# Eight kinds of matrix product written as four side-by-side strips of 32 output rows, in a two-part attention kernel whose order a planner sets

## The chip, the core and the metric

The kernel runs on one core of one Trainium2 chip. The metric is the device time of one execution in microseconds (us); the time before is the median of three runs. A profile records one further execution, instruction by instruction, on the core's engines: TensorE (PE, with the weight loads apart as PEld), VectorE (DVE), ScalarE (ACT), GpSimd (POOL), and SyncE (SP), whose queue issues most of the transfers.

## The reference

Two independent halves read their own `x` of 2048 rows by 512 columns, and their outputs are placed side by side. Half A is softmax attention with 32 query heads of width 16 that share one key and one value head. Half B is linear attention with a softmax feature map.

```
A:  q = x @ wq  (32 heads x 16),  k = x @ wk,  v = x @ wv  (16 columns each)
    p = softmax(q k^T / 4) over 2048 keys;   out_A = (p @ v) @ wo
B:  q, k, v = x @ wqkv  (32 heads x 16 each)
    phi(t) = [softmax(t w_phi), softmax(-t w_phi)]         (32 features per head)
    kv = phi(k)^T v,  z = sum of phi(k) over the rows
    out_B = (phi(q) kv / (phi(q) z + 1e-6)) @ wo
out = [out_A, out_B]
```

Half A holds nearly all of the work: 32 heads x 2048 x 2048 exponentials.

## The kernel before

**Half A, scores.** A unit is 128 keys against 512 queries of one head. Its score product has a contraction over 32 rows (16 of them hold zeros for the other head of a pair), so four units stand in the four row strips of the array side by side (`score`, line 1694, called "row" form below). Four units with the same keys block make a quad; there are 512 quads. A quad takes one of two ways:

- The ACT way (371 quads). Units are gathered into score groups of three and of two in turn (`next_qk`, `qk`); three PSUM banks hold a group of three and two others a group of two. One ACT instruction does the exponentials of a whole group, 128x1536 or 128x1024 (`expo`, line 1758), and frees its banks for the group after next. Then `pv` (line 1803) multiplies a quad by the values: four products with 32 output rows each, side by side in the column strips ("col" form).
- The DVE way (141 quads). DVE turns the scores into half-precision bit patterns (`bits`, line 1867, one 128x512 piece for each unit), derives three shifted copies of a quad (line 1886 on DVE, line 1883 on POOL, where POOL's copy waits for DVE's copies of the same quad), and `d_sums` (line 1924) sums them with the values in 16 col-form products. The program of a DVE quad is `next_dq` and `d_pv`.

**Half B and the projections.** These are products with all 128 rows and 128 columns of the array ("full" form), four accumulating steps of 512 columns each, or two for `b_q4`: `proj_q` (line 1684, 15 times), `outproj` (line 1992, 12), `b_pk` (line 2158, 16), `b_projv` (line 2187, 16), `b_pq` (line 2255, 16), `b_q4` (line 2325, 16), `b_s8` (line 2342, 16). Each writes one of two or three spare PSUM banks; DVE copies the result away, or ACT applies an exponential (line 2166 for keys, line 2262 for queries, twice for each bank).

**What sets the order.** A planner in the kernel (`run`, `ready`, `issue`) keeps a clock for each engine, gives every job a duration, a form, a due time and a priority, and writes the instructions of all engines in the order of its plan. The chip gets each engine's list in that order, and semaphores between them. The planner charges 0.105 us where a TensorE job's form differs from the one before (`SWITCH`). It also follows how busy TensorE was lately (`active`, `weight`) and puts in products of zeros (`fill`, line 1450, and `company`, line 1433), which accumulate nothing, where it holds TensorE for too idle. `SEEDS` has a number for each 14 us of the plan: it jitters the priorities there (`rank`) and chooses some of the planner's thresholds.

**The end.** The last query block's result is finished in `finish_last`: after the last `pv` a chain of two shuffles on DVE, logarithm and exponential on ACT, a product on DVE, the last products with `wo` (lines 2012 and 2049), copies, and three transfers. DVE and SP branch there on a flag that says whether the inputs were in range.

Of the kernel before, what the change touches and what calls it, by code (L numbers as in the profile page):

```python
# [1174 lines left out]
class _Fast:  # L1175
# [180 lines left out]
    def issue(self, j, start):  # L1356
# [79 lines left out]
    def fill(self, cols=(512,), start=False, mode="full", bank=None):  # L1436


        ps, zero = self.ps, self.zero
        if bank is None:  # L1440
            bank = self.ACC
        r, m = (32 if mode == "row" else 128), (32 if mode == "col" else 128)

        def fn(pe):
            mm = None
            for n in cols:
                rhs = self.ones[0:r].unsqueeze(1).to_broadcast([r, n // 128, 128])
                for x in range(0, 128 if mode == "col" else 32, 32):
                    kw = {} if mode == "full" else dict(tile_position=(0, x))
                    mm = pe.matmul(ps[x:x + m, bank, 0:n].rearrange("p (a n) -> p a n", n=128), lhsT=zero[0:r, 0:m], rhs=rhs, start=start, stop=start, **kw)  # L1450
# [105 lines left out]
    def jobs_a(self):  # L1556
# [28 lines left out]
        for qt in range(12):  # L1585
            job(("op", qt), "pe", 0.87, (lambda qt: (lambda: self.outproj(qt)))(qt), mode="full", nb=1, prio=3.5, after=[("on", qt // 4 * 8 + a) for a in range(1, 8, 2)])
            job(("oa", qt), "dve", 0.60, (lambda qt: (lambda: self.outproj2(qt)))(qt), after=[("op", qt)], frees=[("op", qt)], prio=1)
# [87 lines left out]
    def proj_q(self, ch):  # L1675
# [306 lines left out]
    def outproj(self, qt):  # L1982

        ps, On = self.ps, self.On
        P = qt // 4 * 4
# [3 lines left out]
        def fn(pe):  # L1989
            mm = None  # L1990
            for A in range(4):
                mm = pe.matmul(ps[:, bank, :], lhsT=On[:, (P + A) % 6, q0:q0 + 128], rhs=self.wo2[:, A, :], start=(A == 0), stop=(A == 3))  # L1992
            return mm
# [95 lines left out]
    def jobs_b(self, t0, t1):  # L2089
# [12 lines left out]
        for st in range(16):  # L2102
            job(("bk", st), "pe", 0.87, self.b_pk, after=[("wfc", 1, dc) for dc in range(4)] + ([("kv", st - 2)] if st > 1 else []), mode="full", nb=1, prio=3, rel=at(st))
# [4 lines left out]
            job(("bv", st), "pe", 0.87, self.b_projv, after=[(self.BVA, st)], mode="full", nb=1, prio=3)  # L2108
            job(("vs", st), "dve", 1.13, self.b_vs, after=[("bv", st), ("rs", st)], frees=[("bv", st)], prio=1)
# [3 lines left out]
        for m in range(4):  # L2113
            for G in range(4):
                w = [("s8", 4 * (m - 2) + i) for i in range(4)] if m > 1 else [("wf", k, dc) for k in range(2) for dc in range(4)] if m == 0 else []
                job(("bq", m, G), "pe", 0.87, self.b_pq, after=[("wfc", 0, dc) for dc in range(4)] + w, mode="full", nb=1, prio=3,
                    rel=at(15 + 4.5 * m + G))
# [10 lines left out]
            for C in range(4):  # L2128
                job(("q4", m, C), "pe", 0.44, self.b_q4, after=[("ew", m, s) for s in range(2)], mode="full", nb=1, prio=3, rel=at(19 + 4.5 * m + 0.5 * C))
                job(("q4d", m, C), "dve", 0.60, self.b_q4d, after=[("q4", m, C)], frees=[("q4", m, C)], prio=1)  # L2130
        for st in range(16):
            m = st // 4
            job(("s8", st), "pe", 0.87, self.b_s8, after=[("q4d", m, C) for C in range(4)], mode="full", nb=1, prio=3, rel=at(20 + 4.5 * m + 0.9 * (st % 4)))
            job(("s8c", st), "dve", 0.60, self.b_s8c, after=[("s8", st)], frees=[("s8", st)], prio=1)
# [16 lines left out]
    def b_pk(self, st):  # L2151
# [3 lines left out]
        def fn(pe):  # L2155
            mm = None
            for dc in range(4):
                mm = pe.matmul(ps[:, bank, :], lhsT=xT[:, dc, st * 128:(st + 1) * 128], rhs=w[:, dc, :], start=(dc == 0), stop=(dc == 3))
            return mm
# [20 lines left out]
    def b_projv(self, st):  # L2180
# [3 lines left out]
        def fn(pe):  # L2184
            mm = None
            for dc in range(4):
                mm = pe.matmul(ps[:, bank, :], lhsT=xT[:, dc, st * 128:(st + 1) * 128], rhs=w[:, dc, :], start=(dc == 0), stop=(dc == 3))  # L2187
            return mm
# [59 lines left out]
    def b_pq(self, m, G):  # L2248
# [3 lines left out]
        def fn(pe):  # L2252
            mm = None
            for dc in range(4):
                mm = pe.matmul(ps[:, bank, :], lhsT=w[:, dc, G * 128:G * 128 + 128],  # L2255
                               rhs=xT[:, dc, m * 512:(m + 1) * 512], start=(dc == 0), stop=(dc == 3))
            return mm
# [59 lines left out]
    def b_q4(self, m, C):  # L2317
# [3 lines left out]
        def fn(pe):  # L2321
            mm = None
            for sg in range(2):
                G = 4 * sg + C
                mm = pe.matmul(ps[:, bank, :], lhsT=KVn[:, G, :], rhs=ET[:, (8 * m + G) % 16, :], start=sg == 0, stop=sg == 1)  # L2325
            return mm
# [7 lines left out]
    def b_s8(self, st):  # L2334
# [4 lines left out]
        def op(pe):  # L2339
            mm = None  # L2340
            for C in range(4):
                mm = pe.matmul(ps[:, bank, :], lhsT=ET[:, (8 * m + C) % 16, i * 128:i * 128 + 128], rhs=self.Bwo[:, C, :], start=(C == 0), stop=(C == 3))
# [21 lines left out]
    SEG = 14.0  # L2364
    SEEDS = (984051, 95131, 273450, 658257, 663488, 424264, 0, 164647, 270549, 733254, 842970, 0, 1027032, 574002, 1003492, 900138, 838487,
# [3 lines left out]
    PVN = 2  # L2369
# [227 lines left out]
```

## Time and profile before

| | |
|---|---|
| median of three runs | 722.78 us (722.75 to 723.17) |
| time of the profiled execution | 722.69 us |
| its span, first to last instruction | 720.9 us |
| mean granted TensorE clock | 0.999 |
| ACT busy | 707.5 us, 98% of the span |
| PE busy | 679.1 us, 94% |
| DVE busy | 667.0 us, 93% |
| POOL busy | 397.2 us, 55% |

Busy time alone does not say which engine sets the end: three engines are above 90%. ACT's instructions overlap at their ends, and PE's busy time holds the products of zeros. A row `L1758 ACT ACTIVATE f_PT<-f_ps` is the exponential of line 1758, which reads the PSUM tile `f_ps` and writes `f_PT`. A shape such as `128*32 128x512` stands for a product with 128 contraction rows and 32 columns of the array, over 512 columns of the moving operand. In the chain of waits a piece gives its start, its length, and what stood there; in a timeline, the bracket at a row's end is the idle time of that engine ahead of it, with what ended it.

### The profile page before, as it was taken

What the parts mean: (1) busy time and instruction counts of PE and PEld (TensorE: products, weight loads), DVE (VectorE), ACT (ScalarE), POOL (GpSimd) and SP (SyncE); (2) the same over time, 40 slices, a digit from 0 to 9 for tenths busy, and PEclk for the clock granted to TensorE, in tenths of its full rate; (3) what the DMA queues carried; (4) which work ended last, traced back from release to release, by engine and by line L of the source; (5) the groups of instructions that cost most, each with busy time, mean ns of one, the idle gap of its engine ahead of it and who ended that gap; (6) DMA issues with size and microseconds to landing.
All of it is one profiled execution on the core that took longest, in us unless ns stands there. A gap on an engine that the chain in (4) does not pass through costs nothing.

```text
span 720.9 us, 17413 instructions
## 1 busy us (share of the span) xinstructions
PE 679.1 (94%) x7415; PEld 214.6 (30%) x7415; DVE 667.0 (93%) x1101; ACT 707.5 (98%) x666; POOL 397.2 (55%) x291
## 2 busy tenths in 40 slices
PE   9989999999999999999999999999999999999997
PEld 3223323333332232222233222323232232232322
DVE  4999999999999999998999999999999999899995
ACT  6999999999999999999999999999999999999996
POOL 6455646646454564666546456566464466444551
PEclk9999999999999999999999999999999999999999
DMA  9920000000000100000012310100003010040101
GB/s 184 152 79 25 3 9 17 1 25 2 10 17 27 29 2 10 16 3 24 3 42 49 83 38 2 40 9 16 17 2 100 21 43 13 4 118 2 25 30 35
DMA packets 45539, 23.91 MB, mean 33 GB/s; under 512 B 35405, under 2 KB 41549, under 8 KB 45453
## 3 DMA queue, kind: packets, MB, share of 16 engines
q1 hardware_dynamic: 43724, 22.43, 13.5%
q8 instruction: 59, 0.97, 0.6%
q10 hardware_dynamic: 1728, 0.30, 0.2%
q14 instruction: 28, 0.22, 0.1%
HBM read 10.27 MB, written 4.96 MB: 21 GB/s over the span
## 4 chain that ended last, share of the span: by engine, by line
ACT 96%; PE 3%; DMA 1%; DVE 0%; issue 0%
ACT f_PT L1758 91%; ACT f_ET L2262 2%; ACT f_Ek L2166 2%; DMA f_AxT<-in_A_x_dram 1%; PE f_ps L1694 1%; PE f_ps L1924 1%; PE f_ps L2012 1%; PE f_ps L1803 0%; PE f_ps L1992 0%; PE f_ps L1621 0%; DVE f_outA L1456 0%; PE f_ps L1607 0%; PE f_ps L2325 0%; PE f_ps L2049 0%; PE f_ps L1450 0%
## 5 line engine op out<-in xcount | busy, mean ns | idle before, releaser
L1758 ACT ACTIVATE f_PT<-f_ps 128x1536 bf16<-128x1536 f32 x594 | 682.1, 1391 | 0.8 <-PE f_ps L1694 0.7
L1883 POOL TENSOR_TENSOR f_Zt<-f_Z,f_step 128x1024 int32<-128x1024 int32 x187 | 353.7, 1892 | 285.4 <-DVE f_Zt L1886 262.9
L1867 DVE TENSOR_SCALAR f_Z<-f_ps 128x512 int16<-128x512 f32 x564 | 366.4, 681 | 22.2 <-PE f_ps L1694 18.6
L1694 PE MATMUL f_ps<-f_QA,f_KR 32*128 32x512 bf16 x2048 | 300.0, 384 | 32.8 <-ACT f_PT L1758 23.1
L1886 DVE TENSOR_SCALAR f_Zt<-f_Z 128x2048 int16<-128x2048 int16 x236 | 164.0, 717 | 0.2
L1694 PEld LDWEIGHTS f_ps<-f_QA,f_KR 32*128 32x128 bf16 x2048 | 78.1, 91 | 273.7 <-ACT f_PT L1758 187.0
L1803 PE MATMUL f_ps<-f_PT,f_VA 128*32 128x512 bf16 x1484 | 122.2, 386 | 0.4 <-DVE f_accS L1456 0.3
L1924 PE MATMUL f_ps<-f_Zt,f_VK 128*32 128x512 f16 x1692 | 115.7, 379 | 0.0
L1450 PE MATMUL f_ps<-f_ones,f_zero 128*128 128x512 bf16 (+10 forms) x248 | 59.7, 350 | 1.3 <-POOL f_zero L1476 1.3
L1924 PE MATMUL f_ps<-f_Z,f_VK 128*32 128x512 f16 x564 | 56.3, 389 | 0.1
L1924 PEld LDWEIGHTS f_ps<-f_Zt,f_VK 128*32 128x32 bf16 x1692 | 45.1, 97 | 31.5
L1803 PEld LDWEIGHTS f_ps<-f_PT,f_VA 128*32 128x32 bf16 x1484 | 26.7, 94 | 58.5 <-issue 55.0
L1433 PE MATMUL f_ps<-f_ones,f_zero 32*128 32x512 bf16 x75 | 26.9, 380 | 0.0
L1450 PEld LDWEIGHTS f_ps<-f_ones,f_zero 128*128 128x128 bf16 (+2 forms) x248 | 17.0, 97 | 26.6 <-issue 22.2
L1924 PEld LDWEIGHTS f_ps<-f_Z,f_VK 128*32 128x32 bf16 x564 | 14.5, 93 | 33.5 <-issue 29.5
L1456 DVE COPY f_accS<-f_ps 128x512 f32<-128x512 f32 x31 | 21.3, 686 | 3.4 <-PE f_ps L1924 2.2
L1980 POOL TENSOR_TENSOR f_On<-f_accS,f_denS 128x512 bf16<-128x512 f32 x14 | 17.8, 1272 | 6.4 <-DVE f_Zt L1886 4.5
L2262 ACT ACTIVATE f_ET<-f_ps 128x512 bf16<-128x512 f32 x32 | 20.8, 816 | 0.0
L2166 ACT ACTIVATE f_Ek<-f_ps 128x512 bf16<-128x512 f32 x32 | 20.3, 787 | 0.0
L2172 DVE TENSOR_REDUCE f_ssum<-f_Ek 128x64 f32<-128x1024 bf16 x16 | 19.4, 1210 | 1.0 <-ACT f_Ek L2166 0.9
L2197 DVE TENSOR_TENSOR f_vS<-f_ps,f_rs 128x1024 bf16<-128x1024 f32 x16 | 19.5, 1219 | 0.6 <-PE f_ps L2187 0.6
L2255 PE MATMUL f_ps<-f_BxT,f_Wq 128*128 128x512 bf16 x64 | 16.6, 382 | 0.4 <-DVE f_Z L1867 0.2
(108 smaller groups left out, 324.8 us busy)
## 6 DMA issues: line engine op xcount, KB each, us to landing
f_denS<-f_dd SPq DMA_DIRECT2D x15, 256.0 KB
out_dram<-f_outB SPq DMA_DIRECT2D x17, 128.0 KB, 2.3
f_Wk<-f_wd SPq DMA_DIRECT2D x4, 512.0 KB
f_Ek<-f_wd SPq DMA_DIRECT2D x4, 512.0 KB
f_accS<-f_accS SPq DMA_DIRECT2D x60, 32.0 KB
out_dram<-f_outA SPq DMA_DIRECT2D x14, 128.0 KB, 1.8
f_Bwv<-in_B_wqkv_dram SPq DMA_DIRECT2D x1, 512.0 KB
f_Bwo<-in_B_wo_dram SPq DMA_DIRECT2D x1, 512.0 KB
```

The lines of the kernel that those rows point to most:

```text
L1433: self.add("pe", lambda pe: pe.matmul(out, lhsT=zero[0:32, :], rhs=rhs, start=False, stop=False, tile_position=(0, 0)), reads=["ones", "ze ...
L1450: mm = pe.matmul(ps[x:x + m, bank, 0:n].rearrange("p (a n) -> p a n", n=128), lhsT=zero[0:r, 0:m], rhs=rhs, start=start, stop=start, **kw)
L1456: self.add("dve", lambda v: v.tensor_copy(out=out, in_=in_), reads=reads, writes=writes)
L1694: return pe.matmul(self.ps[:, bank, :], lhsT=self.KR[32 * g:32 * g + 32, sc % 2, kap * 128:(kap + 1) * 128], rhs=self.QA[32 * g:32 * g + 3 ...
L1758: self.add("act", lambda a: a.activation(out=PT[:, sl[0]:sl[0] + size, :], in_=ps[:, b0:b0 + size, :], func=ACT.Exp), reads=[("PS", b0 + i ...
L1803: mm = pe.matmul(ps[32 * g:32 * g + 32, bank, :], lhsT=w, rhs=PT[:, slots[g], :], start=start, stop=stop, tile_position=(0, 32 * g))
L1867: self.add("dve", lambda v: v.tensor_scalar(out=o, in0=ps[:, bank, :], scalar1=self.Z1, scalar2=self.Z0, op0=ALU.mult, op1=ALU.add), reads ...
L1883: self.add("pool", lambda g: g.tensor_tensor(out=w(Zt[:, t - 1]), in0=w(Z), in1=step.to_broadcast([128, 256 * (b - a)]), op=ALU.add), read ...
L1886: self.add(eng, lambda v: v.tensor_scalar(out=Zt[:, t - 1, a:b], in0=Z[:, a:b], scalar1=256.0 * t, scalar2=None, op0=ALU.add), reads=zk, w ...
L1924: mm = pe.matmul(ps[32 * g:32 * g + 32, bank, :], lhsT=w[:, k, :], rhs=Zf[k][:, sl[g], :], start=start and k == 0, stop=stop and k == 3, t ...
L2166: self.add("act", (lambda a, sg: (lambda e: e.activation(out=Ek[:, r, a].rearrange("p h f -> p (h f)"), in_=ps[:, bank, :], func=ACT.Exp, ...
L2262: self.add("act", lambda e: e.activation(out=self.ET[:, sl, :], in_=self.ps[:, bank, :], func=ACT.Exp, scale=sg), reads=[("PS", bank)], wr ...
```

## The change

A helper `strips` replaces the one product of 128 output rows by four of 32 output rows. Strip `g` loads columns 32g to 32g+31 of the old weights, reads the same moving operand as the others, and writes partitions 32g to 32g+31 of the same bank, at column strip `g` of the array. All seven functions named above for the projections and half B use it, and the planner is told that their form is col. The key projections, the first query projection, the value projections of half A (line 1654), the folding of `w_phi` (line 2143) and the last products with `wo` stay full. Durations in the plan are the same. `last_full` now counts these jobs by name. `SEEDS` has other numbers, so the order differs nearly everywhere.

```diff
-            if j.mode == "full" and j.name[0] != "fill":
+            if j.name[0] != "fill" and (j.mode == "full" or j.name[0] in ("pq", "op", "bk", "bv", "bq", "q4", "s8")):
                 self.last_full = start
...
+    def strips(self, pe, bank, lhsT, rhs, start, stop):
+
+        for g in range(4):
+            mm = pe.matmul(self.ps[32 * g:32 * g + 32, bank, :], lhsT=lhsT[:, 32 * g:32 * g + 32], rhs=rhs, start=start, stop=stop, tile_position=(0, 32 * g))
+        return mm
...
-            job(("pq", ch), "pe", 0.87, (lambda ch: (lambda: self.proj_q(ch)))(ch), mode="full", nb=1, prio=0 if ch == 0 else 2.2,
+            job(("pq", ch), "pe", 0.87, (lambda ch: (lambda: self.proj_q(ch)))(ch), mode="col", nb=1, prio=0 if ch == 0 else 2.2,
...
             for dc in range(4):
-                mm = pe.matmul(ps[:, bank, :], lhsT=self.wq[:, dc, A * 128:A * 128 + 128], rhs=xT[:, dc, qc * 512:(qc + 1) * 512], start=(dc == 0), stop=(dc == 3))
+                mm = self.strips(pe, bank, self.wq[:, dc, A * 128:A * 128 + 128], xT[:, dc, qc * 512:(qc + 1) * 512], dc == 0, dc == 3)
             return mm
...
     SEG = 14.0
-    SEEDS = (984051, 95131, 273450, 658257, 663488, 424264, 0, 164647, 270549, 733254, 842970, 0, 1027032, 574002, 1003492, 900138, 838487,
+    SEEDS = (984051, 95131, 956796, 0, 157941, 1040273, 775127, 200086, 678638, 373812, 58605, 447202, 227563, 908490, 615953, 565535, 941748,
...
```

The other six functions and their jobs are edited in the same way. Line numbers in the changed file are 6 higher from line 1455 on (5 from `b_pq` on): scores are line 1700, `pv` is 1809, `d_sums` is 1930, all strips are line 1458.

The instruction lists hold the same ACT, DVE, POOL and SP work before and after, with one order for another; ACT has 297 groups of three, 296 of two and one of one in both. On PE the products on the taken path go from 7415 to 8606. Counted in these lists by the array form of each product, the changes of form from one PE product to the next go from 1071 to 1007, and the products listed above that follow col-form work directly from 32 to 43.

Three places of the lists follow. The first is PE, at the products with `wo` (`f_wo,f_On`) for the third block of 512 queries; `f_QA,f_KR` are scores, `f_PT,f_VA` is `pv`, `f_VK` is `d_sums`. Before:

```order
L1803 MATMUL f_ps<-f_PT,f_VA 32x512 x4
L1992 MATMUL f_ps<-f_wo,f_On 128x512 x4
L1694 MATMUL f_ps<-f_QA,f_KR 128x512 x4
L1803 MATMUL f_ps<-f_PT,f_VA 32x512 x4
L1694 MATMUL f_ps<-f_QA,f_KR 128x512 x2
L1803 MATMUL f_ps<-f_PT,f_VA 32x512 x4
L1992 MATMUL f_ps<-f_wo,f_On 128x512 x4
L1694 MATMUL f_ps<-f_QA,f_KR 128x512 x4
L1924 MATMUL f_ps<-f_Z,f_VK 32x512 x4
L1924 MATMUL f_ps<-f_Zt,f_VK 32x512 x12
```

and changed:

```order
L1700 MATMUL f_ps<-f_QA,f_KR 128x512 x3
L1458 MATMUL f_ps<-f_wo,f_On 32x512 x16
L1700 MATMUL f_ps<-f_QA,f_KR 128x512 x3
L1809 MATMUL f_ps<-f_PT,f_VA 32x512 x8
L1700 MATMUL f_ps<-f_QA,f_KR 128x512 x7
L1450 MATMUL f_ps<-f_ones,f_zero 128x256
L1458 MATMUL f_ps<-f_wo,f_On 32x512 x16
L1700 MATMUL f_ps<-f_QA,f_KR 128x512 x4
L1930 MATMUL f_ps<-f_Z,f_VK 32x512 x4
L1930 MATMUL f_ps<-f_Zt,f_VK 32x512 x12
```

Before, each of the two products stood right behind a `pv`; now each stands behind scores or a filling product.

The second place is the last ten rows of PE's list; `f_wo,f_On` are here the last query block's products with `wo`. Before:

```order
L1694 MATMUL f_ps<-f_QA,f_KR 128x512 x3
L1924 MATMUL f_ps<-f_Z,f_VK 32x512 x4
L1924 MATMUL f_ps<-f_Zt,f_VK 32x512 x12
L1694 MATMUL f_ps<-f_QA,f_KR 128x512
L1924 MATMUL f_ps<-f_Z,f_VK 32x512 x4
L1924 MATMUL f_ps<-f_Zt,f_VK 32x512 x12
L2012 MATMUL f_ps<-f_wo,f_On 128x512
L1803 MATMUL f_ps<-f_PT,f_VA 32x512 x12
L2012 MATMUL f_ps<-f_wo,f_On 128x512 x10
L2049 MATMUL f_ps<-f_wo,f_On 128x512 x4
```

and changed:

```order
L1700 MATMUL f_ps<-f_QA,f_KR 128x512
L2018 MATMUL f_ps<-f_wo,f_On 128x512
L1809 MATMUL f_ps<-f_PT,f_VA 32x512 x4
L1930 MATMUL f_ps<-f_Z,f_VK 32x512 x4
L1930 MATMUL f_ps<-f_Zt,f_VK 32x512 x12
L1809 MATMUL f_ps<-f_PT,f_VA 32x512 x4
L2018 MATMUL f_ps<-f_wo,f_On 128x512 x10
L2055 MATMUL f_ps<-f_wo,f_On 128x512 x2
L2018 MATMUL f_ps<-f_wo,f_On 128x512 x2
L2055 MATMUL f_ps<-f_wo,f_On 128x512 x2
```

Behind the last DVE quad stand 4 products of `pv` where there were 12. Ahead of these rows, from the score group that is the sixth from last, the changed list runs: scores 4, half B's strips 16, scores 2, DVE quad, scores 3, `pv` 4, scores 2, `pv` 4, `wo` 3, scores 3, `pv` 4, DVE quad. So a product of half B (`b_s8`, the last) has moved into the end, and the products of zeros that stood there before are gone.

The third place is DVE at the end. Before:

```order
L1867 TENSOR_SCALAR f_Z<-f_ps 128x512 x2
L1886 TENSOR_SCALAR f_Zt<-f_Z 128x2048 x2
L2537 BRANCH_PREFETCH_HINT
L1886 TENSOR_SCALAR f_Zt<-f_Z 128x2048 x2
L2541 TENSOR_LOAD flag
L2544 COMPARE_AND_BRANCH
L1970 STREAM_SHUFFLE f_denS<-f_denS 128x512
L1978 SCALAR_TENSOR_TENSOR f_On<-f_accS,f_evn,f_denS 128x512
```

and changed:

```order
L1873 TENSOR_SCALAR f_Z<-f_ps 128x512 x4
L2542 BRANCH_PREFETCH_HINT
L1959 RECIPROCAL f_denC<-f_denC 128x16
L1873 TENSOR_SCALAR f_Z<-f_ps 128x512
L2546 TENSOR_LOAD flag
L2549 COMPARE_AND_BRANCH
L1462 CAST f_outB<-f_ps 128x512
L1892 TENSOR_SCALAR f_Zt<-f_Z 128x2048 x5
L1976 STREAM_SHUFFLE f_denS<-f_denS 128x512
L1984 SCALAR_TENSOR_TENSOR f_On<-f_accS,f_evn,f_denS 128x512
```

Before, the last four `f_Zt` copies came straight behind the last `f_Z` and ahead of the branch; now the branch and a copy of half B's output (of the strips that moved into the end) come first, and five `f_Zt` copies follow. In both programs the last copy on POOL waits for the last of DVE's `f_Zt` copies, and the last DVE quad on PE waits for POOL's copy.

More of the change, by code (lines that the diff above doesn't have):

```diff
@@ L1585, in jobs_a @@
         for qt in range(12):
-            job(("op", qt), "pe", 0.87, (lambda qt: (lambda: self.outproj(qt)))(qt), mode="full", nb=1, prio=3.5, after=[("on", qt // 4 * 8 + a) for a in range(1, 8, 2)])
+            job(("op", qt), "pe", 0.87, (lambda qt: (lambda: self.outproj(qt)))(qt), mode="col", nb=1, prio=3.5, after=[("on", qt // 4 * 8 + a) for a in range(1, 8, 2)])
             job(("oa", qt), "dve", 0.60, (lambda qt: (lambda: self.outproj2(qt)))(qt), after=[("op", qt)], frees=[("op", qt)], prio=1)
@@ L1991, in fn @@
             for A in range(4):
-                mm = pe.matmul(ps[:, bank, :], lhsT=On[:, (P + A) % 6, q0:q0 + 128], rhs=self.wo2[:, A, :], start=(A == 0), stop=(A == 3))
+                mm = self.strips(pe, bank, On[:, (P + A) % 6, q0:q0 + 128], self.wo2[:, A, :], A == 0, A == 3)
             return mm
@@ L2102, in jobs_b @@
         for st in range(16):
-            job(("bk", st), "pe", 0.87, self.b_pk, after=[("wfc", 1, dc) for dc in range(4)] + ([("kv", st - 2)] if st > 1 else []), mode="full", nb=1, prio=3, rel=at(st))
+            job(("bk", st), "pe", 0.87, self.b_pk, after=[("wfc", 1, dc) for dc in range(4)] + ([("kv", st - 2)] if st > 1 else []), mode="col", nb=1, prio=3, rel=at(st))
             job(("fe", st), "act", 0.955, self.b_ek, after=[("bk", st)], frees=[("bk", st)], prio=0)
@@ L2107, in jobs_b @@
             job(("vt", st), "pool", 0.52, self.b_vt, after=[("rs", st)] + ([("kv", st - 2)] if st > 1 else []), prio=1.0)
-            job(("bv", st), "pe", 0.87, self.b_projv, after=[(self.BVA, st)], mode="full", nb=1, prio=3)
+            job(("bv", st), "pe", 0.87, self.b_projv, after=[(self.BVA, st)], mode="col", nb=1, prio=3)
             job(("vs", st), "dve", 1.13, self.b_vs, after=[("bv", st), ("rs", st)], frees=[("bv", st)], prio=1)
@@ L2115, in jobs_b @@
                 w = [("s8", 4 * (m - 2) + i) for i in range(4)] if m > 1 else [("wf", k, dc) for k in range(2) for dc in range(4)] if m == 0 else []
-                job(("bq", m, G), "pe", 0.87, self.b_pq, after=[("wfc", 0, dc) for dc in range(4)] + w, mode="full", nb=1, prio=3,
+                job(("bq", m, G), "pe", 0.87, self.b_pq, after=[("wfc", 0, dc) for dc in range(4)] + w, mode="col", nb=1, prio=3,
                     rel=at(15 + 4.5 * m + G))
@@ L2128, in jobs_b @@
             for C in range(4):
-                job(("q4", m, C), "pe", 0.44, self.b_q4, after=[("ew", m, s) for s in range(2)], mode="full", nb=1, prio=3, rel=at(19 + 4.5 * m + 0.5 * C))
+                job(("q4", m, C), "pe", 0.44, self.b_q4, after=[("ew", m, s) for s in range(2)], mode="col", nb=1, prio=3, rel=at(19 + 4.5 * m + 0.5 * C))
                 job(("q4d", m, C), "dve", 0.60, self.b_q4d, after=[("q4", m, C)], frees=[("q4", m, C)], prio=1)
@@ L2132, in jobs_b @@
             m = st // 4
-            job(("s8", st), "pe", 0.87, self.b_s8, after=[("q4d", m, C) for C in range(4)], mode="full", nb=1, prio=3, rel=at(20 + 4.5 * m + 0.9 * (st % 4)))
+            job(("s8", st), "pe", 0.87, self.b_s8, after=[("q4d", m, C) for C in range(4)], mode="col", nb=1, prio=3, rel=at(20 + 4.5 * m + 0.9 * (st % 4)))
             job(("s8c", st), "dve", 0.60, self.b_s8c, after=[("s8", st)], frees=[("s8", st)], prio=1)
@@ L2157, in fn @@
             for dc in range(4):
-                mm = pe.matmul(ps[:, bank, :], lhsT=xT[:, dc, st * 128:(st + 1) * 128], rhs=w[:, dc, :], start=(dc == 0), stop=(dc == 3))
+                mm = self.strips(pe, bank, xT[:, dc, st * 128:(st + 1) * 128], w[:, dc, :], dc == 0, dc == 3)
             return mm
@@ L2186, in fn @@
             for dc in range(4):
-                mm = pe.matmul(ps[:, bank, :], lhsT=xT[:, dc, st * 128:(st + 1) * 128], rhs=w[:, dc, :], start=(dc == 0), stop=(dc == 3))
+                mm = self.strips(pe, bank, xT[:, dc, st * 128:(st + 1) * 128], w[:, dc, :], dc == 0, dc == 3)
             return mm
@@ L2254, in fn @@
             for dc in range(4):
[L2255 to L2256 removed]
+                mm = self.strips(pe, bank, w[:, dc, G * 128:G * 128 + 128], xT[:, dc, m * 512:(m + 1) * 512], dc == 0, dc == 3)
             return mm
@@ L2324, in fn @@
                 G = 4 * sg + C
-                mm = pe.matmul(ps[:, bank, :], lhsT=KVn[:, G, :], rhs=ET[:, (8 * m + G) % 16, :], start=sg == 0, stop=sg == 1)
+                mm = self.strips(pe, bank, KVn[:, G, :], ET[:, (8 * m + G) % 16, :], sg == 0, sg == 1)
             return mm
@@ L2341, in op @@
             for C in range(4):
-                mm = pe.matmul(ps[:, bank, :], lhsT=ET[:, (8 * m + C) % 16, i * 128:i * 128 + 128], rhs=self.Bwo[:, C, :], start=(C == 0), stop=(C == 3))
+                mm = self.strips(pe, bank, ET[:, (8 * m + C) % 16, i * 128:i * 128 + 128], self.Bwo[:, C, :], C == 0, C == 3)
             return mm
```

6 rows, old and new, of the table SEEDS are left out of this document.

## The prediction

> **What bounds the kernel now.** I read the page first: the chain of waits, and the busy shares.
>
> ```profile
> PE 679.1 (94%) x7415; PEld 214.6 (30%) x7415; DVE 667.0 (93%) x1101; ACT 707.5 (98%) x666; POOL 397.2 (55%) x291
> ...
> PEclk9999999999999999999999999999999999999999
> ...
> ACT 96%; PE 3%; DMA 1%; DVE 0%; issue 0%
> ```
>
> Three engines are busy above 90%, but the chain that ended last lies on ACT for 96% of the span. To see whether ACT has any slack, I took its instructions by shape, and pieces of the chain in order of time (start, length, what, count).
>
> ```profile
> L1758 ACT ACTIVATE f_PT<-f_ps 128x1536 bf16<-128x1536 f32 x297 | 476.1, 1603 | 0.8 <-PE f_ps L1694 0.7
> L1758 ACT ACTIVATE f_PT<-f_ps 128x1024 bf16<-128x1024 f32 x296 | 349.5, 1181 | 0.0
> L2262 ACT ACTIVATE f_ET<-f_ps 128x512 bf16<-128x512 f32 x32 | 20.8, 816 | 0.0
> L2166 ACT ACTIVATE f_Ek<-f_ps 128x512 bf16<-128x512 f32 x32 | 20.3, 787 | 0.0
> ```
>
> ```profile
> 8.30 63.40 ACT f_PT L1758 x56
> 71.70 0.98 ACT f_Ek L2166 x2
> 72.68 1.34 ACT f_PT L1758
> ...
> 388.14 109.62 ACT f_PT L1758 x97
> ...
> 628.00 76.06 ACT f_PT L1758 x67
> ```
>
> The means of the groups (1603 and 1181 ns) overlap their neighbours, so the pace comes from the chain: 56 instructions, 28 of each size, in 63.40 us are 2.26 us for a pair; 97 in 109.62 and 67 in 76.06 give the same 2.26 within 0.01. One of 128x1536 takes 1.34, so one of 128x1024 takes 0.92, and two of half B's take 0.98. Summed: 296 pairs x 2.26 = 668.96, one more large one 1.34, the last group of one unit about 0.49 (half of 0.98), 32 x 0.98 = 31.36; together 702.15. ACT starts its exponentials at 8.30, so without any stall they would end at 710.45. They do end at 711.33:
>
> ```profile
> 688.93 22.40 ACT L1758 ACTIVATE f_PT<-f_ps 128x1536 bf16<-128x1536 f32 x20
> ```
>
> ```profile
> ACT f_PT L1758 <- PE f_ps L1694: 0.7, 1, 0.7
> ```
>
> The first row is from ACT's timeline (688.93 + 22.40 = 711.33), the second from the list of waits (total, times, longest): ACT waited for scores once, for 0.7 us. All that ACT loses to TensorE in the whole execution is thus 0.7 to 0.9 us. The rest of the span is 8.30 us ahead, which the change doesn't touch, and 9.6 us behind (711.33 to 720.9), the end.
>
> **What the strips cost.** Prices of stretches on PE are in the chain where it crosses PE:
>
> ```profile
> 585.89 0.33 PE f_ps L1803 x4
> 586.22 0.97 PE f_ps L1992 x4
> ...
> 589.79 0.98 PE f_ps L1924 x16
> ...
> 591.43 0.54 PE f_ps L2325 x2
> ...
> 706.76 0.55 PE f_ps L1803 x8
> ...
> 708.86 0.32 PE f_ps L1694 x3
> ```
>
> One `pv` quad between two other forms takes 0.33, two take 0.55, so a quad in a row of its own form takes 0.22 and the change of form 0.11. Four full products take 0.97 = 4 x 0.215 + 0.11. Sixteen col products in four steps (line 1924, the form that the strips will have, with two-byte operands as theirs) take 0.98. So a four-step projection costs 0.97 before and 0.98 changed where it stands between scores: nothing is gained there. Where it follows col work, the change of form goes: `pv` and a projection cost 0.33 + 0.97 = 1.30 before, and 0.33 + 0.87 = 1.20 changed. Over the list, changes of form go from 1071 to 1007; 64 x 0.11 = 7 us less of PE's time.
>
> What are 7 us of PE worth? PE spends far more on nothing:
>
> ```profile
> L1450 PE MATMUL f_ps<-f_ones,f_zero 128*128 128x512 bf16 (+10 forms) x248 | 59.7, 350 | 1.3 <-POOL f_zero L1476 1.3
> L1433 PE MATMUL f_ps<-f_ones,f_zero 32*128 32x512 bf16 x75 | 26.9, 380 | 0.0
> ```
>
> 60 + 27 us are products of zeros. So the 7 us lie beside ACT's stream and are worth, at most, the 0.7 to 0.9 us of stalls. Those lie in one place, 585.5 to 592.35, where the chain leaves ACT and runs through PE: the first place shown of the lists, two products with `wo` right behind `pv` quads, then a `b_q4` behind another. There I count three changes of form that strips would save (0.33 us). In the changed order this bundle doesn't stand any more: both products with `wo` stand behind scores or zeros. I take 0.3 off for the stalls. The bounds: at best all of the 0.9 goes; at worst the new order has stalls of its own (a rival below).
>
> More weight loads: 4 become 16 for a projection.
>
> ```profile
> L1924 PEld LDWEIGHTS f_ps<-f_Zt,f_VK 128*32 128x32 bf16 x1692 | 45.1, 97 | 31.5
> L1992 PEld LDWEIGHTS f_ps<-f_wo,f_On 128*128 128x128 bf16 x48 | 3.7, 98 | 5.7 <-DVE f_Z L1867 1.5 <-issue 0.7 <-DVE f_mq L1642 0.2
> ```
>
> A narrow load's record is as long as a wide one's (97 against 98 ns), but four of them overlap: 16 products with their loads fit in the 0.98 above, where 16 x 97 ns one after another would be 1.55. I cost them at nothing; their cover is the streaming of the product before. The bounds: 0, and 1.55 - 0.98 = 0.57 us for each projection if the cover were gone; the row of 16 is the nearest, as it is the same shape.
>
> [...]
>
> **The end.** Now from the score group that is the sixth from last. Before, PE's rows and DVE's:
>
> ```profile
> 704.09 1.35 DVE L1867 TENSOR_SCALAR f_Z<-f_ps 128x512 int16<-128x512 f32 x2 [0.19 <-PE f_ps L1694]
> 704.11 0.11 PEld L1694 LDWEIGHTS f_ps<-f_QA,f_KR 32*128 32x128 bf16 x4 [0.35 <-ACT f_PT L1758]
> ...
> 705.36 2.49 DVE L1886 TENSOR_SCALAR f_Zt<-f_Z 128x2048 int16<-128x2048 int16 x4
> ...
> 707.93 1.89 POOL L1883 TENSOR_TENSOR f_Zt<-f_Z,f_step 128x1024 int32<-128x1024 int32 x1 [3.42 <-DVE f_Zt L1886]
> 709.29 0.01 DVE L1970 LOAD_MASK_SELECT f_denS<-f_denS  x1 [1.44 <-issue]
> ```
>
> ```profile
> 711.46 0.32 PE f_ps L2012
> 711.78 0.76 PE f_ps L1803 x12
> 712.54 2.27 PE f_ps L2012 x10
> ```
>
> That score group starts at 704.11, released by ACT, and the last `pv` ends at 712.54; everything behind hangs on it and has the same parts in both programs. Changed, PE alone, from 704.11: six runs of scores at 0.33 (1.98), the strips 0.98, a DVE quad behind scores 0.98 and two behind `pv` 0.87 each (1.74), `pv` four times behind another form and once behind col (4 x 0.33 + 0.22 = 1.54), three products with `wo` 0.76 (3 x 0.216 + 0.11) and one 0.32: 8.30, so the last `pv` ends at 712.41, 0.13 earlier.
>
> But the last DVE quad also waits for DVE and POOL. The last `f_Z` starts about 704.1 as before and ends at 704.8, since there is one where there were two (1.35 / 2 each). The copy of half B's output waits for the strips: 704.11 + 0.33 + 0.98 = 705.4, then 0.69; five `f_Zt` at 2.49 / 4 = 0.62 make 3.1; to 709.3. POOL's copy starts 0.08 later as before (707.93 against 705.36 + 2.49 = 707.85) and takes 1.89: 711.3. PE would come to that quad at 712.41 - 0.22 - 0.87 = 711.32. The two meet, so I take 0 for the end. The bounds: -0.13 where DVE is earlier, and, if the branch that now stands ahead of DVE's copies costs all of the 1.44 us that DVE idled behind it before, the copy starts at 706.25 instead of 705.4, and the end is 0.85 later.
>
> **Sum.** 722.69 (the profiled execution's own time, 0.09 under the median of the runs) - 0.3 (stalls) + 0 (end) = 722.4 for that execution, and 722.5 beside the median; I say 722.4. With the bounds of the terms, -0.9 - 0.1 and +0.85: 721.7 to 723.5.
>
> **The rivals.**
>
> *The new order stalls ACT (slower).* I counted, from the lists and the prices above, the stretches of more than 1.25 us of other work between two score groups: 47 before, 58 changed, since the planner now puts a projection behind a `pv` more often (43 against 32). Each stretch must fit while ACT works on the group ahead (0.92 or 1.34 us) with one more group in store. For: there are more of them. Against: 47 of them cost 0.9 us in all before, 0.02 each. If each of the 11 new ones cost 0.2 us, the time would be 722.69 + 2.2 = 724.9. It decides from 0.13 us for each of the 11. Chance 0.08.
>
> *Strips cost more than full products (slower).* If their loads were not covered, 91 projections x 0.57 and 16 of two steps x 0.28 are 56 us of PE time; the zeros could give way for part of it, but each long stretch would stand ahead of a score group. If a quarter reached ACT: 722.7 + 14 = 737. Against it stand the stretches of 16 narrow products at 0.98, of which the program before has 141. Chance 0.03. [...]
>
> *PE was the bound (faster).* Then the 7 us saved come off: 715.7. Against: the 87 us of zeros, and ACT's single wait of 0.7. Chance 0.02.
>
> *All stalls go and the end gains too.* 722.69 - 0.9 - 0.13 = 721.7: the low end of my own range, not another case.
>
> **Chances.** A measurement of this kernel tells about 0.2% from no change: 1.45 us, so 721.3 and 724.2. My forecast, no change within that, has 0.85; the two slower cases 0.11; the faster one 0.02, and 0.02 for a start or an end that is shorter than I can account for. So faster 0.04, same 0.85, slower 0.11. The range: 721.5 to 723.7, which takes in the bounds of the terms, and leaves out the rivals.
>
> **What would show it.** In the changed profile: 16 products of line 1458 between scores in 0.97 to 0.99 us, and 0.87 behind `pv`; ACT's pairs at 2.26; ACT's waits for scores below 1 us in all; the last exponential at 710.5 to 711.4; the last `pv` within 0.2 of 712.5, released by POOL. The granted clock stays at 0.99 or more, since strips of four fill the array as one full product does; a lower digit in that row would be a cause that I have not priced. I am wrong if ACT's waits for line 1700 sum to more than 2 us, or if the stretch from the last exponential to the end is longer than 10.5 us.

## The result, and the profile after

The changed kernel takes 726.80 us (median of six executions, 725.50 to 727.79); the kernel before takes 722.76 us beside it on the same chip. The ratio is 1.0053, with an interval of 1.0042 to 1.0064: slower, by 4.0 us. The range of the prediction ended at 723.7.

The profiled execution of the changed kernel took 727.72 us, with a span of 726.0 us, 5.0 us more than before (725.97 against 720.95, unrounded). First the page of the changed kernel, the rows that answer to those read before:

```profile
PE 681.3 (94%) x8602; PEld 219.3 (30%) x8606; DVE 665.2 (92%) x1101; ACT 707.7 (97%) x666; POOL 397.8 (55%) x291
...
PEclk9999999999999999999999999999999999999997
...
ACT 91%; PE 4%; DVE 3%; DMA 1%; SPq 0%; issue 0%; DVEq 0%
```

Two things are new: the last slice of the granted TensorE clock has a 7, and ACT's share of the chain fell from 96% to 91%, with DVE now in it. The busy times hardly moved, so the loss is a wait. Next ACT's groups by shape, its list of waits for scores (total, times, longest), and its timeline at the start and at the end:

```profile
L1764 ACT ACTIVATE f_PT<-f_ps 128x1536 bf16<-128x1536 f32 x297 | 477.3, 1607 | 0.8 <-PE f_ps L1700 0.7
L1764 ACT ACTIVATE f_PT<-f_ps 128x1024 bf16<-128x1024 f32 x296 | 350.1, 1183 | 0.0
```

```profile
ACT f_PT L1764 <- PE f_ps L1700: 3.7, 2, 3.0
```

```profile
8.41 61.17 ACT L1764 ACTIVATE f_PT<-f_ps 128x1536 bf16<-128x1536 f32 x54 [0.66 <-PE f_ps L1700]
...
678.84 32.17 ACT L1764 ACTIVATE f_PT<-f_ps 128x1024 bf16<-128x1024 f32 x28
714.05 0.60 ACT L1764 ACTIVATE f_PT<-f_ps 128x512 bf16<-128x512 f32 x1 [3.05 <-PE f_ps L1700]
```

ACT is done with all groups but the last at 678.84 + 32.17 = 711.01. Until then it has waited once for TensorE, for the 0.66 us ahead of its first group, at 8.41; the groups by shape show 0.8 us of idle time in all, so within the stream it loses 0.2 at most. Then it stands for 3.05 us in front of its very last group. So the whole stream of 593 groups runs without a stall, and the loss lies behind 704. The chain of waits (start, length, what, count) shows the same: first three long pieces of ACT, then the end.

```profile
8.41 61.17 ACT f_PT L1764 x54
...
377.15 110.85 ACT f_PT L1764 x98
...
619.02 74.59 ACT f_PT L1764 x66
...
704.49 0.98 PE f_ps L1458 x16
...
707.83 0.69 DVE f_outB L1462
708.52 3.02 DVE f_Zt L1892 x5
711.54 0.04 issue
711.58 1.90 PE f_ps L1930 x16
...
715.10 1.71 PE f_ps L1930 x13
716.81 0.43 PE f_ps L1809 x4
717.24 0.33 issue
717.57 2.26 PE f_ps L2018 x9
```

A pair of ACT still takes 2.26 to 2.27 us (61.17 / 27, 110.85 / 49, 74.59 / 33), and sixteen strips take 0.98 (line 1458). But at 707.83 the chain leaves for DVE, and the last `pv` ends at 717.24, where it ended at 712.54 before: 4.7 of the 5.0 us between the two profiled executions. The other 0.33 is the gap behind it. What happened on DVE and PE:

```profile
704.30 0.69 DVE L1873 TENSOR_SCALAR f_Z<-f_ps 128x512 int16<-128x512 f32 x1
707.83 0.69 DVE L1462 CAST f_outB<-f_ps 128x512 bf16<-128x512 f32 x1 [2.84 <-PE f_ps L1700]
708.44 3.09 DVE L1892 TENSOR_SCALAR f_Zt<-f_Z 128x2048 int16<-128x2048 int16 x5
```

```profile
708.58 0.60 PE L2018 MATMUL f_ps<-f_wo,f_On 128*128 128x512 bf16 x2 [0.52 <-DVE f_outB L1462]
...
709.44 0.40 PE L1809 MATMUL f_ps<-f_PT,f_VA 128*32 128x512 bf16 x4
711.58 0.62 PE L1930 MATMUL f_ps<-f_Z,f_VK 128*32 128x512 f16 x4 [1.75 <-DVE f_Zt L1892]
```

Between the last `f_Z` and the copy of half B's output DVE idles for 2.84 us. The row names scores of line 1700, but what the copy reads are the strips, and these ended at 704.49 + 0.98 = 705.47: the engine named had long been done, so it isn't what DVE waited for. What stands between the two rows in DVE's list is the branch. The five `f_Zt` copies start at 708.44, where the prediction had them at 706.1, and PE idles 0.52 us behind the late copy of half B's output, and 1.75 us more until the last `f_Zt` copy is there. And then PE is slow: from 711.58, sixteen products take 1.90 where they take 0.98 elsewhere. The table by stretches of 2 us says why (stretch, length, busy time of PE, PEld, DVE, ACT and POOL with their instructions, then the granted clock):

```profile
709.00:711.00 2.00, 0.84 (x8) 0.20 (x7) 2.00 (x5) 1.94 (x2) 0.00 (x0) 1.00 0.21 70
711.00:713.00 2.00, 1.42 (x16) 0.46 (x16) 1.97 (x4) 0.01 (x1) 1.39 (x1) 0.51 0.05 12
713.00:715.00 2.00, 2.00 (x18) 0.45 (x14) 1.05 (x1) 0.60 (x1) 0.50 (x1) 0.50 0.01 4
715.00:717.00 2.00, 2.00 (x24) 0.52 (x16) 0.00 (x0) 0.00 (x0) 0.00 (x0) 0.50 0.01 4
717.00:719.00 2.00, 1.67 (x10) 0.77 (x8) 1.21 (x5) 1.16 (x4) 0.00 (x0) 0.78 0.00 0
```

It is halved from 711.04, within the hole, to 717.87, just while the two last DVE quads and `pv` are to run. The theory to test has thus two parts: the branch ahead of DVE's copies delays them, and the hole that this leaves in PE's work then costs the granted clock. The rivals: the strips themselves, the new order as a whole, and a fall of the clock that has nothing to do with the hole.

### The profile page after: what moved, and what is told of

It is laid out like the page before. It is cut to its first block, busy times and chain, and to the rows that moved or that the text cites. A ratio compares the mean times of both kernels' runs of the same rounds, so it can differ in the third digit from the quotient of the medians.

```text
span 726.0 us, 19778 instructions
## 1 busy us (share of the span) xinstructions
PE 681.3 (94%) x8602; PEld 219.3 (30%) x8606; DVE 665.2 (92%) x1101; ACT 707.7 (97%) x666; POOL 397.8 (55%) x291
## 4 chain that ended last, share of the span: by engine, by line
ACT 91%; PE 4%; DVE 3%; DMA 1%; SPq 0%; issue 0%; DVEq 0%
ACT f_PT L1764 87%; ACT f_ET L2267 2%; ACT f_Ek L2172 2%; DVE f_Z L1873 1%; PE f_ps L1930 1%; PE f_ps L1700 1%; DVE f_Zt L1892 1%; DMA f_AxT<-in_A_x_dram 1%; PE f_ps L1809 0%; PE f_ps L2018 0%; PE f_ps L1458 0%; SPq L1473 0%; DVE f_QA L1462 0%; PE f_ps L1450 0%; PE f_ps L2055 0%
## 5 line engine op out<-in xcount | busy, mean ns | idle before, releaser
L1700 PE MATMUL f_ps<-f_QA,f_KR 32*128 32x512 bf16 x2048 | 305.0, 384 | 33.1 <-ACT f_PT L1764 21.6
L1450 PE MATMUL f_ps<-f_ones,f_zero 128*128 128x512 bf16 (+10 forms) x253 | 57.1, 351 | 1.3 <-POOL f_zero L1482 1.3
L1458 PE MATMUL f_ps<-f_BxT,f_Wq 128*32 128x512 bf16 x256 | 16.7, 381 | 0.6 <-DVE f_vS L2203 0.3
```

Source lines behind the costliest of these rows:

```text
L1700: return pe.matmul(self.ps[:, bank, :], lhsT=self.KR[32 * g:32 * g + 32, sc % 2, kap * 128:(kap + 1) * 128], rhs=self.QA[32 * g:32 * g + 3 ...
```

## The experiments

In all of them the time of the kernel before, on the same chip, lay between 722.82 and 723.14 us.

**The branch behind the copies.** One number of the changed kernel: how many of DVE's last steps stand behind the branch.

```diff
-        self.cut["dve"] -= 8 - max(gaps)[1]
+        self.cut["dve"] -= 2
```

> The changed kernel with one edit: DVE's branch on the flag stands behind the five f_Zt copies, with two instructions of DVE left behind it, as in the kernel before; strips and the order of every engine otherwise as changed. Theory B (the branch: DVE gets its next instruction 2.9 us after the branch, and in the changed order the copies that the last DVE quad needs stand behind it): the copies run at 705.5 to 709.2, PE doesn't wait, the last pv ends near 712.5, granted clock 0.999, time 722.2 to 722.9. Rival S (the strips cost PE time) and rival O (the new order itself stalls): 726 to 727 as changed.

Measured: 722.88 us (722.55 to 723.26), ratio 1.0000 (0.9991 to 1.0009). All of the loss is gone. DVE's timeline and the chain's last piece:

```profile
705.75 0.69 DVE L1462 CAST f_outB<-f_ps 128x512 bf16<-128x512 f32 x1 [0.59 <-PE f_ps L1458]
706.36 3.09 DVE L1892 TENSOR_SCALAR f_Zt<-f_Z 128x2048 int16<-128x2048 int16 x5
709.76 0.01 DVE L1976 LOAD_MASK_SELECT f_denS<-f_denS  x1 [0.31 <-DMA f_denS<-f_denC]
```

```profile
712.74 2.26 PE f_ps L2018 x10
```

The copy of half B's output now waits for the strips, as the prediction had it, and DVE idles 0.31 us behind the branch; the row puts that down to a transfer of `f_denS`, so nothing of the branch shows any more. The last `pv` ends at 712.74. So neither the strips nor the new order cost anything that these runs resolve; the place of the branch does.

**Full products in the new order.** The helper issues one product of 128 rows again, the order and the branch stay.

```diff
-        for g in range(4):
-            mm = pe.matmul(self.ps[32 * g:32 * g + 32, bank, :], lhsT=lhsT[:, 32 * g:32 * g + 32], rhs=rhs, ...
+        mm = pe.matmul(self.ps[:, bank, :], lhsT=lhsT, rhs=rhs, start=start, stop=stop)
```

> The changed order, semaphores and branch, but each four strips written as one product of 128 rows again. Theory B: as slow as changed, 725.5 to 727.8, with DVE's next instruction 2.9 us behind its branch. Rival S: back to 722.5. The changes of form that come back (43 x 0.11 us) lie beside ACT's stream and cost at most 0.5.

Measured: 725.59 us (725.18 to 727.03), ratio 1.0038 (1.0026 to 1.005). Slow too, without a strip in it. Here the chain of waits names the branch itself, line 2548 on DVE's queue:

```profile
705.41 0.08 DVEq L2548
705.49 2.85 issue
```

The branch takes 0.08 us, and for 2.85 us behind it DVE has nothing to do that the profile shows.

**Strips in the old order.** The kernel before with its own order, and `strips` in the seven functions (the title says eight kinds; the diff has seven); the planner goes on with full products, and so changes nothing. One of the seven, the others alike:

```diff
-                mm = pe.matmul(ps[:, bank, :], lhsT=On[:, (P + A) % 6, q0:q0 + 128], rhs=self.wo2[:, A, :], start=(A == 0), stop=(A == 3))
+                mm = self.strips(pe, bank, On[:, (P + A) % 6, q0:q0 + 128], self.wo2[:, A, :], A == 0, A == 3)
```

> The order of the kernel before on every engine (its SEEDS, the jobs still planned as full), but the seven products written as strips. Theory B: 722.3 to 722.9, as before, ACT's waits for scores 0.3 to 0.8. Rival S: 725 to 727. Rival O: as before.

Measured: 722.98 us (722.79 to 723.37), ratio 1.0002 (0.9993 to 1.0011). Strips gain and cost nothing beyond the interval, some 0.1%.

**The branch early in the old order.** The kernel before, with its branch ahead of the last four `f_Zt` copies, where it stood right behind them.

```diff
-        self.cut["dve"] -= 8 - max(gaps)[1]
+        self.cut["dve"] -= 6
```

> The kernel before with one edit: DVE's branch stands ahead of the last four f_Zt copies. Theory B: the copies start near 707.9 instead of 705.4, POOL's copy ends near 712.4, the last pv near 714.5 instead of 712.5: time 724.5 to 725, more if the clock falls. Rivals S and O: no change, 722.8.

Measured: 725.27 us (724.87 to 726.83), ratio 1.0036 (1.0023 to 1.0049). The old kernel becomes slow by the same move. DVE's timeline, and where the last `pv` ends, from the chain:

```profile
708.62 2.50 DVE L1886 TENSOR_SCALAR f_Zt<-f_Z 128x2048 int16<-128x2048 int16 x4 [2.81 <-issue]
```

```profile
714.52 0.76 PE f_ps L1803 x12
715.28 2.27 PE f_ps L2012 x10
```

The last `pv` ends 2.74 us later than the 712.54 of before. In this profiled execution (724.96 us) the granted clock stayed at 1.00 through the end, so the delay alone is worth 2.1 us there (724.96 - 722.82); the median is 2.5 above the kernel before.

**Zeros in the hole.** To tell the clock from the delay: the changed kernel with products of zeros on PE ahead of the next-to-last DVE quad. The branch stays early.

```diff
+        if quad == 140:
+            self.fill(cols=(512,) * 14, mode="col")
```

> Edit: the changed kernel, with 14 steps of products of zeros (four strips of 512 columns each, 14 x 0.22 = 3.1 us, adding nothing) written on TensorE ahead of the next-to-last DVE quad, where TensorE idled for 3.8 us (707.75 to 711.58). The branch stays ahead of DVE's copies, so these still start 2.9 us behind it. Theory (two parts: the branch delays the copies by 2.4 us, and the idle stretch that this makes then costs the granted clock): the clock stays at 1.00 through 711 to 717, the two last DVE quads and pv run at full pace, the last pv ends at 714.5 to 714.9 instead of 717.24, the time is 725.0 to 725.5. Rival (the clock isn't what the rest is lost to, or it falls whatever TensorE does there): 0.5 in those stretches, or no shorter tail, 726.5 to 727.8.

Measured: 726.43 us (725.80 to 726.60), ratio 1.0048 (1.0034 to 1.0061). The clock came out as the theory has it; the time lies above the theory's 725.5, just under the rival's 726.5, and the last `pv` ended at 716.40 instead of 714.5 to 714.9. PE's timeline and the clock:

```profile
710.29 3.19 PE L1450 MATMUL f_ps<-f_ones,f_zero 128*32 128x512 bf16 x56
713.32 0.39 PE L1932 MATMUL f_ps<-f_Z,f_VK 128*32 128x512 f16 x4
```

```profile
713.00:715.00 2.00, 2.00 (x34) 0.69 (x26) 1.68 (x1) 0.29 (x1) 1.13 (x1) 1.00 0.03 8
715.00:717.00 2.00, 2.00 (x28) 0.79 (x29) 0.50 (x4) 0.36 (x2) 0.00 (x0) 1.00 0.01 4
```

I had misread the hole. PE isn't idle from 707.75 to 711.58, as the expectation says; it still does two products with `wo`, scores and a `pv` in between, and its holes are the 0.52 and the 1.75 us of the rows above. So the zeros started at 710.29 and ran 1.16 us beyond DVE's last copy, which ended at 712.16. They took back what the clock gave. Hence the same with nine steps:

```diff
-            self.fill(cols=(512,) * 14, mode="col")
+            self.fill(cols=(512,) * 9, mode="col")
```

> Edit: as with the zeros in the gap, with 9 steps of zeros in place of 14. In that run the clock stayed at 1.00 in the whole end, but the zeros, which started at 710.29 and not at 707.75, ran till 713.32, 1.16 us past DVE's last copy (712.16), so they took back what the clock gave. Nine steps of 0.217 end at 712.25. Theory (the delay by the branch is worth about 2.4 us and the clock the rest, and it falls because of TensorE's idle 1.75 us ahead of the next-to-last DVE quad): the clock is 0.999 or 1.000 in every execution, the last pv ends at 715.2 to 715.5, the time is 725.1 to 725.6 with a spread under 1 us (the changed kernel: 725.5 to 727.8). Rival (zeros hold the clock but something else in the end is as long): 726 or more.

Measured: 725.44 us (725.02 to 725.72), ratio 1.0033 (1.0021 to 1.0046). The chain:

```profile
710.28 1.94 PE f_ps L1450 x36
712.22 0.86 PE f_ps L1932 x16
...
715.26 2.26 PE f_ps L2020 x10
```

The clock is 0.998 or above in every execution (I had said 0.999; the kernel before has 0.998 to 1.000 too), the last `pv` ends at 715.26, and the spread is 0.7 us instead of 2.3. The delay is thus worth 725.44 - 722.98 = 2.5 us, and the clock about the rest: 726.80 - 722.76 - 2.5 = 1.5 us in the median. How much it takes changes from one execution to the next. The six of the changed kernel, with their mean granted clock:

```
725.50  1.000      726.57  0.996      727.72  0.994
725.50  0.998      727.03  0.997      727.79  0.995
```

By and large, the lower the clock, the longer the execution. The 725.5 of an execution that lost little clock is the time that nine steps of zeros give to all of them.

**The branch between the copies.** How the price depends on the work ahead of the branch: changed kernel, two of the five copies ahead of it, three behind.

```diff
-        self.cut["dve"] -= 8 - max(gaps)[1]
+        self.cut["dve"] -= 5
```

> Edit: the changed kernel with DVE's branch moved behind the copy of half B's output and the first two of the five f_Zt copies; three of them still stand behind it. Theory (what the branch costs is 2.9 us counted from its own issue, of which the work queued ahead of it hides its own length): the branch is issued at about 706.3, as soon as the copy of half B's output has been let go, the first two copies run till 707.6, the other three start at 709.1 and end at 711.0 (709.45 with the branch behind all five), so the last pv ends 1.5 us later than there, at 714.2; TensorE idles under 2 us, the clock stays at 1.00; time 724.2 to 724.6. Rival 1 (the branch costs its 2.9 us in full wherever copies stand behind it): the last three end at 712.4, time 725.7 or more. Rival 2 (the 1.44 us of the row in the profile before is the whole price): copies end at 710.9 less what is hidden, 709.5 to 709.7, time 722.9 to 723.2.

Measured: 726.64 us (724.91 to 727.39), ratio 1.0046 (1.0032 to 1.006). That is above the theory's 724.2 to 724.6. DVE, PE and the clock:

```profile
706.69 1.28 DVE L1892 TENSOR_SCALAR f_Zt<-f_Z 128x2048 int16<-128x2048 int16 x2
709.96 1.90 DVE L1892 TENSOR_SCALAR f_Zt<-f_Z 128x2048 int16<-128x2048 int16 x3 [1.99 <-issue]
```

```profile
711.91 0.40 PE L1930 MATMUL f_ps<-f_Z,f_VK 128*32 128x512 f16 x4 [1.95 <-DVE f_Zt L1892]
```

```profile
713.00:715.00 2.00, 2.00 (x18) 0.65 (x21) 1.38 (x1) 0.60 (x1) 0.83 (x1) 0.67 0.01 4
715.00:717.00 2.00, 2.00 (x15) 0.47 (x8) 0.69 (x4) 0.26 (x1) 0.00 (x0) 0.50 0.01 4
```

DVE idles 1.99 us: by the records shown below its next instruction comes 3.10 us behind the branch, and for 1.1 of these the two copies still run. That is the theory, against the rival with 2.9 in full. The end of the copies is 711.86 instead of 711.0; 0.33 of it is a later start of the whole end (the copy of half B's output at 706.08 against 705.75), the rest a branch issued 0.3 and a following instruction 0.2 later than I took. But I had said that under 2 us of hole leave the clock alone, and 1.95 us didn't: the clock is halved from 713.7 to 717.1. That part of the expectation was wrong, and by the time alone (over 725.7) rival 1 would have been right; it is DVE's rows that tell the two apart. The execution that kept 0.998 took 724.91 us.

**Full products and a late branch** in the new order complete the pairs.

> Edit: the changed kernel with one full product in place of the four strips everywhere (the order stays), and DVE's branch behind the five f_Zt copies. It completes the pairs: with the branch early this order took 725.6 with full products and 726.8 with strips, with the branch late 722.9 with strips. Theory (strips cost and gain nothing, the whole loss lies in the end): 722.8 to 723.5, at most 0.5 us over strips for the changes of form at places where ACT has no slack; last pv at 712.6 to 713.2. Rival (the new order lives on the strips, which hide changes of form): ACT's stalls of 0.7 us grow by 1.5 or more, 724.4 or longer.

Measured: 723.17 us (722.65 to 723.79), ratio 1.0003 (0.9994 to 1.0012). ACT's waits for scores:

```profile
ACT f_PT L1763 <- PE f_ps L1699: 0.8, 2, 0.7
```

0.66 us of it is again the wait ahead of the first group; the new order doesn't need the strips either. In the profiled execution, the longest of its eleven (723.79 us), the last `pv` ended at 713.58, 0.4 later than I had said. With the branch late both forms take what the kernel before takes, with the branch early both lose 2.8 to 4 us.

**The hint ahead of the branch.** What are the 2.9 us? DVE's list has a hint that announces the branch, two steps ahead of it. Here it stands 24 steps ahead; branch and order are those of the changed kernel.

```diff
-        ahead = dict(pe=24, act=10, dve=2, pool=2, sp=2)
+        ahead = dict(pe=24, act=10, dve=24, pool=2, sp=2)
```

> Edit: the changed kernel, with the hint that announces DVE's branch 24 planned steps ahead of it (some 15 us by the trace) in place of 2 (1.4 us); the branch stays where it is. The question is what the 2.9 us behind the branch are. Theory 1 (they are the wait for the code behind the branch, and the hint comes too late to fetch it ahead): DVE's idle row behind the branch falls from 2.84 to under 1 us, the copies start at about 706, the time is 722.7 to 723.2. Theory 2 (they belong to the branch itself, whatever is announced): the row stays at 2.8 to 3.1, the time at 725.4 to 727.8. For theory 2: where the hint stood 2.75 us ahead (the old order with the branch early) the next instruction still came 2.91 us behind the branch, where it stood 0.76 ahead 3.04 to 3.14; so half the distance in a hint moved it by 0.2. I give theory 2 0.7.

Measured: 722.88 us (722.71 to 723.07), ratio 0.9997 (0.9988 to 1.0006). I had given 0.7 to the other theory. DVE's timeline:

```profile
704.79 0.69 DVE L1873 TENSOR_SCALAR f_Z<-f_ps 128x512 int16<-128x512 f32 x1
706.07 0.69 DVE L1462 CAST f_outB<-f_ps 128x512 bf16<-128x512 f32 x1 [0.59 <-PE f_ps L1458]
706.68 3.09 DVE L1892 TENSOR_SCALAR f_Zt<-f_Z 128x2048 int16<-128x2048 int16 x5
```

With the branch still ahead of it, the copy of half B's output waits only for the strips. The trace's records of DVE's queue give for each kernel how long ahead of the branch the hint was, and how long behind it the first instruction came (us):

```
kernel                           hint ahead   next behind
before                               0.76         3.04
changed                              1.44         2.87
changed, branch late                 0.75         3.14
changed, branch between copies       0.76         3.10
before, branch early                 2.75         2.91
changed, hint early                 16.83         0.62
```

Two rows hold another wait: with the branch late the next instruction also waited for a transfer of `f_denS`, which landed at 709.73, 0.03 us before it started; with the early hint it waited for the strips, so 0.62 is an upper bound. So the 2.9 to 3.1 us behind the branch are a wait that an early hint takes away. That it is a wait for the code behind the branch, as theory 1 has it, is not shown: on q14, whose packets the profile lists as `instruction`, an 8 KB packet starts 1.18 us behind DVE's branch in the kernel before and 1.05 in the changed one, and the records don't say for which engine. A hint 2.75 us ahead does nothing; how early it must be, between 2.75 and 16.8 us, wasn't tried.

None of these kernels beats the one before: with the branch out of the way, ACT's stream and the parts of the end that both share are left.

## Why the prediction was wrong

**What bounds the kernel: right.** ACT's pairs run at 2.26, and its stream runs without stalls up to the end.

**The strips: right.** Sixteen take 0.98 between scores, their loads cost nothing, and PE's saved time is worth nothing that shows: 1.0002 with strips alone, and in the new order with the branch late 1.0000 with strips against 1.0003 without.

**"I take 0.3 off for the stalls": not found.** The list's one wait of 0.7 us was misread as a stall in the stream. ACT's timeline in the kernel before has it ahead of the very first group, at the start that the prediction's sum counts from:

```profile
8.30 63.40 ACT L1758 ACTIVATE f_PT<-f_ps 128x1536 bf16<-128x1536 f32 x56 [0.66 <-PE f_ps L1694]
```

The changed kernel has the same 0.66 at 8.41. Of the 0.8 us of idle time in the quoted rows by shape, the stream before thus had 0.2 at most, the bundle of 585 to 592 included, so there was no 0.3 to win. The 0.88 us between 710.45 and 711.33 lie within the rounding of the pace: 63.40 / 28 is 2.264, and 296 x 0.004 are 1.2 us. With the branch late the bundle is gone and the time is that of before to within 0.1%.

**"I take 0 for the end": the step that failed**, and with it its upper bound, +0.85. The place and the cause were named there (the branch that now stands ahead of DVE's copies), the price was wrong. I read it from the 1.44 us that DVE idled behind the branch before. That row isn't the price; it is what was left of it behind the copies that were still running: the branch was issued 3.04 us ahead of that row's instruction, at 706.25, and two and a half copies ran beside it till 707.85. Moved ahead of the copies, it had nothing to hide it, and cost its 2.9: the copies started 2.3 us after the predicted 706.1, and the time rose by 2.5 us with the clock held. The quoted rows would have bounded it: the branch stood behind copies that started at 705.36, and DVE went on at 709.29, so up to 3.9 us, not up to 1.44. (A slip beside it: 706.1 and five copies of 0.62 give 709.2, not 709.3; nothing hangs on it.)

The branch's own row would have misled further: it takes 0.08 us in the changed kernel, and the next instruction came 2.87 us behind it.

**"The granted clock stays at 0.99 or more": failed too.** On the page's row the last slice went to 7. The text said that a lower digit would be a cause not priced, and it was one: 1.5 us in the median, 2.5 in the profiled execution. It follows from the first miss, since the delay made the hole: with zeros in it the clock held at 0.998 or above. That the clock goes by how far the products fill the array, the reason given, no run shows; with the branch late the strips leave it at 0.999 or more, with the branch early it fell to 0.994, and with full products to 0.996.

**The rivals.** None of them was it. The order did not stall ACT in the stream (the one at 0.08), strips cost nothing (0.03), PE wasn't the bound (0.02). The two marks for being wrong were both met: ACT's waits for line 1700 sum to 3.7 us, and from the last exponential (714.65) to the end of the span (726.0) it is 11.35 us.

## What to carry to other kernels

An idle row behind a branch shows only what the work queued ahead of it did not cover (here 2.84 us with no copy ahead, 1.99 with two); before moving a branch forward, price it from its issue, or bound it by the whole stretch from the first piece of work that may have run beside it. Look at how far ahead of its branch a hint stands in time: here 17 us ahead it made the branch cost nothing, 3 us ahead it did nothing. Before counting an engine's wait as a stall, see where it stands: the 0.7 us here were the start. A hole of nearly 2 us on TensorE near the end came with a halved clock here (1.75 and 1.95 us), worth some 1.5 us in the median of the changed kernel: add that to the price, and let the range be longer on that side.

## What the runs showed of the hardware

- DVE's first instruction behind the branch came 2.87 to 3.14 us after it in these kernels (the 3.14, with five copies ahead, holds a wait for a transfer), and 0.62 us or less after it in the one with an early hint. Copies that had been issued ahead of the branch ran on meanwhile and hid it: DVE idled 2.84 with none ahead, 1.99 with two, and with five, 3.1 us in all, only 0.31, for the transfer.
- The granted clock fell to half with holes on PE of 1.75 us (changed, and with full products) and 1.95 us (branch between the copies), for 6.83 us in the changed kernel and 3.4 in the two others. The clock records of the two kernels that don't reach the end of the trace are 713.386 us long (before) and 706.559, 6.827 and 6.827 us (changed), whole multiples of 3.4133 (209, 207, 2, 2). In the 3.41 us right ahead of the fall PE's records show 1.72 us of idle time in the changed kernel (707.62 to 711.04, so the fall came within the hole), 1.83 with full products, and 1.65 with the branch between the copies. In the old order with the branch early the hole was 1.63 us, and the clock stayed in that profiled execution. Whether the length of one hole decides or the idle time in the stretch ahead is not shown, nor why like executions lost between nothing and 2.3 us.
- Beside POOL's copy (711.61 to 713.50 in the changed kernel), DVE's product for `f_On` took 1.81 us, where it took 0.75 in the kernel before, which had it behind that copy; it lay on no path that set the end.
